# A fused linear-attention, gated-MLP and channel-mix kernel: normalisation sums without the mean, four outputs completed by a matmul with the identity, the gelu table loaded first, a branch hint, and a new hand-written order

## The chip, the cores and the metric

One core of one Trainium2 chip. The metric is the device time of one execution in microseconds, the median of several runs; lower is better. A second number is the span of one profiled execution: from its first to its last instruction.

## What is computed

Three layers follow each other on (batch 2, 768 tokens, 384 features). All inputs are float32 or, for the weights, float64, which arrive as pairs of 32-bit words; the results must hold to float32.

```python
for t in range(S):                                   # attention, 8 heads of 48
    y[:, :, t] = r_t @ (state + (u * k_t) v_t^T)     # u: the "present token's part"
    state = w_t[:, None] * state + k_t v_t^T
h = gelu_tanh(x @ w_in);  u, v = halves of h         # gated MLP, 2 x 512
v_n = (v - mean(v)) / sqrt(var(v) + 1e-6) * g_ln
x = x + (u * (w_sg @ v_n + b_sg)) @ w_out
k = relu(mix_k(x, x_prev) @ w_k) ** 2                # channel mix, 1024 wide
out = sigmoid(mix_r(x, x_prev) @ w_r) * (k @ w_v)
```

If some input lies outside the ranges for which the fast form is exact, a flag is set and a slow general form (`general`) runs after it; with the inputs used here it does not run.

## The kernel before

**Tiles.** Tokens are cut into four groups of 384 (g = 0 to 3; two batches times two halves). Attention works on 16 units (a group and a pair of heads) and 12 packs (a group and a third of its features, decays and keys). Chunks of 128 tokens are handled by matmuls; the state is carried by scans on VectorE (DVE). Every matmul of the later layers is done three times, with the high and low parts of its operands (`mm3`, lines 196 to 198), to keep float32 precision: so ScalarE (ACT) casts a high part of each operand and DVE subtracts to get the low part.

**Order.** Nothing is scheduled by the compiler: the string `ORDER` is a list of tokens, each token is one small step (`act`, line 624), and each engine runs its instructions in the order in which the tokens stand. A token names a step and the unit, pack, weight piece or tile it works on: for instance `L` loads a pack's decays, `6` moves 16 rows of a pack into the tile `six` by two DMAs (line 286), `T A P S I J` are the attention matmuls of a unit, `n` the present token's part (DVE, `t1 = pa * vT`), `O` the store of a unit (`store`, line 400), `o` six small DMAs that share a unit's rows among three features (`xT<-t1`, lines 404 and 405), `v` and `u` the first MLP matmul and its gelu, `M` the second (over tokens), `W` the third, `E`, `R`, `Z` the channel mix. `e` is a matmul on zeros and ones whose result nobody reads; it only keeps TensorE at work. All DMAs are issued by the queue of SyncE (SP), one after the other.

**Unit's output.** `outer` (I) opens a PSUM tile `py` and adds the state's part, `inner` (J) adds the part inside a chunk, and `store` (O) adds `t1` on DVE while it moves `py` to SBUF.

**Normalisation.** `mm1_v` is one generator, stepped by its token: matmuls; gelu on ACT with the row sum; on GpSimd (POOL) the sum is turned into minus the mean (line 439); ACT squares with that as its bias (line 442) and sums; POOL makes the factor by a power (lines 443 to 445); ACT applies it (line 450); ACT casts the high part into `vn_hi` (line 452); DVE makes `vn_lo`. `vn_hi` and `vn_lo` are one buffer for both batches: the second batch's casts wait until the first batch's last `M` has read it, and `M` of the second batch needs six of them.

**PSUM.** `v`, `u`, `M`, `W`, `E` and `e` share three buffers, so a matmul group waits until ACT or DVE has emptied the one three before it.

**End.** After the last output, the flag columns are summed (line 659), reduced by a matmul and compared (line 663); each engine loads the flag into a register (line 665) and branches (line 667) past the body of `general`, which holds over a thousand instructions, to a block of semaphore settings and the closing barriers.

Of the kernel before, what the change touches and what calls it, by code (L numbers as in the profile page):

```python
# [36 lines left out]
ORDER = """L1 L0 e C0.l e q0 e V0 e Q e D1 C3.l e w0 e D0 p1 q1 e e C1.l a0 p0 e C0.x j0 e C0.b e g0 e e e e C0.t e f0 e d0 e e C0.h e C0.r e K0 A0 C0.q  # L37
a1 C0.o 60 j1 g1 e e e e m0 f1 P0 C3.x T0 n0 C3.b V1 k0 e C3.t w1 e S0 K1 C3.h L2 d1 q2 P1 c0 C2.l C1.x T1 61 s0 C1.b A1 x0 C3.o n1 k1 C1.t e
V2 I0 m1 C1.r C1.h S1 C1.q D2 J0 c1 C1.o p2 s1 w2 e O0 e L3 x1 e a2 e K2 e e j2 C2.x e g2 P2 I1 C2.b f2 d2 J1 C2.t 62 n2 C2.r T2 C2.h D3 V3
C2.q A2 w3 O1 k2 L4 C3.r a3 S2 C2.o q3 p3 j3 m2 C3.q P3 C8.l c2 g3 A3 s2 T3 f3 n3 x2 D4 e e e k3 e m3 I2 p4 a4 S3 K3 j4 J2 d3 c3 P4 g4 w4 L5  # L40
T4 s3 V4 f4 q4 C8.x A4 p5 O2 k4 C4.l C8.b x3 S4 m4 c4 e C8.t I3 D5 C8.h J3 s4 n4 x4 63 C8.o e e d4 p6 e I4 w5 a5 V6 O3 A5 q5 j5 C4.x g5 o3 T5
C4.b f5 J4 m5 k5 C4.t S5 O4 C4.r w6 C4.h K4 e C4.q e C6.l C4.o e P5 K5 64 c5 d5 X0.1.h P6 L6 X0.2.h s5 C5.l X0.0.h A6 65 n6 x5 X0.1.l T6 V5
m6 I5 k6 C6.x X0.2.l S6 C6.b J5 c6 X0.0.l C6.t s6 w7 C6.h e e q6 C5.x p7 T7 C6.o x6 C5.b A7 n5 k7 C5.t P7 O5 C5.h C5.r m7 S7 C5.q C7.l I6
C5.o L7 c7 D6 V7 v0.2 C6.r s7 C6.q C9.l q8 K6 p8 x7 a6 C7.x j6 C7.b J6 g6 v0.2 v0.0 w8 C7.t f6 d6 C7.h C7.r n7 v0.2 C10.l C9.x O6 A8 q7 C7.q
C9.b V8 P8 C7.o v0.0 m8 I7 C8.r D7 C8.q C23.l T8 C9.t v0.0 a7 J7 C10.x j7 C10.b p9 g7 C9.r v0.1 66 k8 C9.q C10.t C11.l K7 C9.h C10.r w9 d7
C10.h L8 S8 C10.q n8 67 A9 C23.h C9.o c8 C10.o P9 q10 v0.0 O7 V10 s8 v0.2 u0.0 o7 v0.0 C11.x m9 v0.2 x8 v0.0 u0.1 D8 u0.0 v0.1 C11.b T9 K8
u0.1 C11.t I8 p10 a8 v0.2 k9 C11.h S9 j8 C11.r C23.o v0.1 J8 C11.o g8 C11.q u0.3 w10 O8 c9 f8 d8 f7 P10 s9 68 u0.3 A10 x9 n10 T10 V9 m10 v0.1
C24.l I9 k10 p11 v0.1 A11 v0.1 J9 n9 S10 C24.x V11 O9 P11 w11 m11 c10 L9 T11 q9 s10 L11 u0.2 C24.b x10 C16.l C24.t n11 k11 V13 C24.r I10
C15.l X1.0.h D9 u0.2 C13.l S11 X1.2.h X1.0.l J10 p12 c11 a9 X1.2.l X1.1.h v1.0 s11 C24.q X1.1.l x11 j9 K9 g9 C16.h P12 v1.0 C16.o u1.3 d9 f9
C15.h L10 O10 q11 C15.o v1.0 I11 w12 D11 C22.l C13.h T12 u1.3 C13.o J11 k12 D10 u1.2 69 O11 p13 K10 o11 v1.0 K11 P13 a10 u1.2 j10 g10 v1.0  # L50
S12 C22.h v1.1 n13 c12 a11 d10 f10 V12 w13 s12 610 C22.o A13 x12 j11 v1.0 C21.l P14 v1.1 m13 p14 T13 n12 A12 g11 k13 V14 v1.1 C20.l S13 m12 B
I12 C21.h c13 d11 u1.1 f11 s13 C21.o x13 A14 u1.1 J12 v1.1 C20.h T14 O12 w14 v1.1 C17.l m14 u1.0 k14 n14 v1.1 V15 I13 u1.0 C25.l C20.o 611
S14 C17.h J13 C17.o c14 C26.l v1.2 s14 w15 C18.l O13 x14 C25.x C25.b p15 C25.t T15 C25.r X2.1.h C29.l P15 C25.q X2.1.l k15 v2.1 X2.2.h n15
C18.h X2.2.l X2.0.h C18.o v1.2 X2.0.l C12.l A15 v2.1 S15 m15 I14 v1.2 v2.0 c15 C12.h s15 v2.1 C12.o x15 C14.l J14 I15 v1.2 O14 v2.0 v2.2 v1.2
C14.h v1.2 v2.1 C14.o J15 v2.0 C30.l v2.2 M0.3 O15 o15 v2.2 v2.0 M0.1 M0.3 | M0.3 C24.h C25.h C24.o C25.o C26.x C29.x C26.b C29.b v2.2 C26.t
C29.t u2.2 C26.h M0.1 C29.h C26.r C26.o M0.1 C26.q C19.l C29.o u2.1 C30.x u2.2 C30.b C30.t C30.h M0.2 C30.o u2.1 C19.h C19.o C27.l M1.2 M0.2
M0.2 C27.x C27.b C27.t C27.h C27.r C27.o C27.q C28.l M1.3 M1.2 M1.2 C28.x C28.b M1.0 C28.t M1.3 C28.h C28.r C28.o M1.3 C28.q C31.l C29.r
C29.q C32.l C30.r u2.0 M1.0 C30.q C33.l C31.x M1.0 C31.b M0.0 u2.0 C31.t C32.x C31.r C32.b C31.h C34.l C31.q C32.t C31.o C32.h C33.x C32.r
C32.o C32.q C38.l C33.b C33.t u2.3 M0.0 C33.r C33.h C34.x C35.l M0.0 C33.q C33.o M1.1 u2.3 C34.b C38.x X3.2.h C34.t X3.1.h C38.b C34.h X3.2.l
C34.r C38.t X3.0.h C39.l X3.1.l C34.q X3.0.l C38.h v3.2 C34.o v2.2 M1.1 v2.1 C35.x v2.2 v2.0 v2.1 u3.1 v3.2 C38.o M1.1 C39.x C35.b v3.1 C39.b  # L60
u3.1 C35.t C39.t v3.2 v2.0 C35.h C35.r C35.o v3.0 C39.h C36.l C35.q C39.o v3.1 u3.0 v3.2 C36.x v3.0 C36.b u3.3 C36.t v3.1 C36.r v3.2 C37.l
u3.2 v3.0 v3.2 G0.3.h G0.0.h G0.3.l C36.h G0.0.l u3.0 C36.o v3.1 C37.x u3.3 C37.b v3.1 C37.t v3.0 v3.1 C37.h v3.0 C37.o G0.1.h v3.0 C36.q
G0.1.l M3.3 u3.2 C37.r G0.2.h C42.l C37.q G0.2.l C38.r C38.q C41.l W0.0 C39.r M3.3 C39.q C40.l C42.x M3.3 C42.b C42.t M3.2 C41.x C42.h W0.0
C42.o C41.b C40.x C41.t C40.b C41.h C40.t C41.o C40.h M2.2 C40.r M3.2 C40.q C43.l C40.o M3.2 C41.r C41.q C44.l C42.r C42.q C45.l M2.1 M2.2
C43.x M2.2 C43.b C44.x C43.t C44.b C43.r C44.t C43.h C49.l C43.q W0.1 C43.o M2.1 C44.h C44.r C45.x M2.1 C44.q C47.l C45.b C44.o C45.t M3.1
W0.1 C45.r C45.h C49.x C46.l C45.q C49.b C45.o C49.t C47.x C49.h C47.b C49.o C47.t C47.h M2.0 M3.1 C47.o M3.1 C46.x C46.b C46.t C46.r C46.h
C48.l C46.q W0.2 C46.o M2.0 C47.r M2.0 C47.q C59.l M3.0 W0.2 G1.3.h G1.2.h C48.x G1.3.l G1.0.h C48.b G1.1.h C59.x G1.2.l C59.b C48.t C59.t
C48.r G1.0.l M2.3 C48.h C51.l C48.q M3.0 C59.h C48.o C49.r M3.0 C49.q C50.l C59.o G1.1.l C51.x C51.b W1.1 M2.3 C51.t C50.x C51.h H0 W1.0 W1.1
Y0.0.0.a Y0.0.2.a Y0.0.0.b Y0.0.1.a Y0.0.2.b W1.2 Y0.0.0.c Y0.0.1.b Y0.0.2.c Y0.0.1.c C50.b W1.0 E0.1 G2.0.h W1.2 G2.1.h C50.t G2.2.h
Y0.1.2.a C50.h E0.7 G2.1.l C50.r Y0.1.2.b C52.l C50.o C50.q M2.3 Y0.1.2.c E0.1 E0.3 G2.3.h C51.o E0.1 E0.7 G2.3.l C51.r E0.1 C53.l E0.7 E0.2  # L70
C51.q C52.x E0.1 E0.7 C52.b E0.3 E0.7 E0.0 C52.t E0.2 G2.0.l C52.h C53.x C52.r C52.o C53.b C52.q C54.l E0.6 E0.2 C53.t E0.2 G2.2.l C53.r E0.2
C53.h C55.l W2.0 C53.q Y0.1.0.a E0.6 C53.o Y0.1.0.b C54.x E0.6 Y0.1.0.c E0.6 W2.2 C54.b E0.6 W2.0 E0.0 C54.t E0.0 C54.h C54.r C55.x W2.1 E0.3
E0.0 C58.l C54.q W2.2 E0.0 E0.3 C55.b E0.3 Z0.0 C55.t G3.0.h W2.1 C55.r G3.2.h G3.0.l C56.l G3.1.h Y0.1.1.a E0.4 C55.h G3.1.l G3.3.h G3.2.l
Y0.1.1.b C55.q G3.3.l Z0.1 Y0.1.1.c E0.4 C55.o E0.4 C58.x E0.4 W3.0 H1 C58.b E0.4 C58.t Z0.2 W3.0 C58.h Y1.0.0.a C58.o Y1.1.0.a W3.1 C56.x
Y1.0.2.a C56.b Y1.1.2.a C56.t Z0.3 Y1.0.1.a C56.r C56.h W3.1 C57.l C56.q Y1.1.1.a E0.5 C54.o C56.o Z0.4 C57.x Y1.0.0.b C57.b E0.5 Y1.0.0.c
# [833 lines left out]
```

## Time and profile before

| | us |
|---|---|
| median of 3 runs | 361.02 (359.25 to 364.27) |
| the profiled execution | 361.11 |
| its span | 359.3 |
| TensorE busy in the span | 332.5 |
| DVE busy | 259.6 |
| ACT busy | 207.5 |

The profiled execution is 1.8 us longer than its span. A row "start us, us" of a timeline is the start from the span's beginning and the length of a merged stretch; in square brackets stands how long the engine was idle before it and what ended that. `PEld` is TensorE's weight load, and an engine's name with a q its sequencer, which waits, branches and issues.

### The profile page before, as it was taken

To read this page: it belongs to the slowest core of one execution; us is meant where nothing else is said; L and a number is where in the kernel's file an instruction comes from. 1 tells how busy PE (TensorE), PEld (TensorE's weight loads), DVE (VectorE), ACT (ScalarE), POOL (GpSimd) and SP (SyncE) were. 2 spreads that over 40 slices of the span, in tenths; PEclk is the share of its full clock that TensorE was granted. 3 is DMA by queue.
4 is the path that set the end of the run, shared out by engine and by line. 5 is a ranking of instruction groups with operands and counts; after the bars stand their busy time and mean duration, and the time that the engine had idled before them with its cause. 6 is when DMAs were issued, how large, how long until landed. Compare 5 with 4: busy or idle time off the path is not lost.

```text
span 359.3 us, 6219 instructions
## 1 busy us (share of the span) xinstructions
PE 332.5 (93%) x2166; PEld 295.5 (82%) x2171; DVE 259.6 (72%) x579; ACT 207.5 (58%) x572; POOL 40.8 (11%) x103
## 2 busy tenths in 40 slices
...
GB/s 212 206 141 188 152 207 160 214 106 167 175 134 185 102 54 31 44 163 37 58 89 88 85 57 44 47 42 31 117 23 53 0 2 66 0 2 44 24 44 33
DMA packets 22440, 32.57 MB, mean 91 GB/s; under 512 B 2944, under 2 KB 18816, under 8 KB 22400
## 3 DMA queue, kind: packets, MB, share of 16 engines
...
q14 instruction: 21, 0.17, 0.1%
...
## 4 chain that ended last, share of the span: by engine, by line
PE 62%; DVE 14%; DMA 10%; ACT 7%; issue 3%; SPq 1%; POOL 1%; DVEq 0%; ACTq 0%
PE po L550 9%; PE ps L198 5%; PE ps L196 5%; PE ps L197 5%; PE pk L198 4%; PE pk L197 4%; PE pk L196 4%; PE po L196 4%; PE po L198 4%; PE po L197 4%; DMA six<-pk 3%; DMA wt<-in_wp_dram 2%; DVE pk L271 2%; DMA vT<-in_rkv_dram 2%; PE pr L196 2%
## 5 line engine op out<-in xcount | busy, mean ns | idle before, releaser
L196 PE MATMUL ps<-wsg,vn_hi 128*128 128x384 f32 x96 | 32.8, 341 | 3.1 <-ACT uT L460 1.8
L198 PE MATMUL ps<-wsg,vn_lo 128*128 128x384 f32 x96 | 32.6, 339 | 0.1
L197 PE MATMUL ps<-wsg,vn_hi 128*128 128x384 f32 x96 | 32.5, 338 | 0.0
L198 PE MATMUL pk<-xk_hi,wk_lo 128*128 128x384 f32 x96 | 32.4, 337 | 0.0
L197 PE MATMUL pk<-xk_lo,wk_hi 128*128 128x384 f32 x96 | 32.3, 336 | 0.0
L196 PE MATMUL pk<-xk_hi,wk_hi 128*128 128x384 f32 x96 | 32.3, 336 | 0.0
L524 DVE TENSOR_TENSOR kr<-kr 128x384 f32<-128x384 f32 x32 | 17.7, 556 | 14.4 <-ACT kr L522 13.9
L529 ACT CAST kk_hi<-kr 128x384 fp32r<-128x384 f32 x32 | 16.1, 513 | 20.7 <-PE po L550 14.5
L522 ACT ACTIVATE kr<-pk 128x384 f32<-128x384 f32 x32 | 15.6, 489 | 18.0 <-PE pk L198 15.6
L553 DVE TENSOR_TENSOR rr<-po,rr 128x384 f32<-128x384 f32 x12 | 6.5, 555 | 25.5 <-PE po L198 14.1
L550 PE MATMUL po<-pl_win_hi,kk_hi 128*128 128x384 f32 x81 | 23.0, 338 | 0.0
L196 PEld LDWEIGHTS ps<-wsg,vn_hi 128*128 128x128 f32 x96 | 18.0, 188 | 3.9 <-ACT uT L460 2.1
L382 ACT COPY sx<-sc 48x144 f32<-48x144 f32 x32 | 14.5, 454 | 8.9 <-DVE sc L376 8.7
L531 DVE TENSOR_TENSOR kk_lo<-kr,kk_hi 128x384 fp32r<-128x384 f32 x32 | 17.4, 555 | 2.6 <-ACT kk_hi L529 2.2
L550 PE MATMUL po<-pl_win_lo,kk_hi 128*128 128x384 f32 x63 | 18.4, 339 | 0.0
L198 PEld LDWEIGHTS ps<-wsg,vn_lo 128*128 128x128 f32 x96 | 18.0, 188 | 0.4 <-DVE vn_lo L454 0.4
L550 PE MATMUL po<-pl_win_hi,kk_lo 128*128 128x384 f32 x54 | 18.2, 338 | 0.0
L198 PEld LDWEIGHTS pk<-xk_hi,wk_lo 128*128 128x128 f32 x96 | 18.0, 188 | 0.0
L197 PEld LDWEIGHTS pk<-xk_lo,wk_hi 128*128 128x128 f32 x96 | 18.0, 188 | 0.0
L196 PEld LDWEIGHTS pk<-xk_hi,wk_hi 128*128 128x128 f32 x96 | 18.0, 188 | 0.0
L197 PEld LDWEIGHTS ps<-wsg,vn_hi 128*128 128x128 f32 x96 | 18.0, 188 | 0.0
L365 DVE TENSOR_TENSOR am<-pA,c_sb 128x768 f32<-128x768 f32 x16 | 15.1, 947 | 3.6 <-PE pA L335 3.6
...
## 6 DMA issues: line engine op xcount, KB each, us to landing
...
```

The lines of the kernel that those rows point to most:

```text
L196: T.matmul(ps, lh, rh, start=(i == 0), stop=False)
L197: T.matmul(ps, lh, rl, start=False, stop=False)
L198: T.matmul(ps, ll, rh, start=False, stop=(i == n - 1))
L271: V.tensor_mul(pk4, pk4, u.rk.rearrange("p two (c j) -> p two c j", c=NCB))
L365: V.tensor_mul(u.am.rearrange("p h (c t) -> p h c t", c=NCB), u.pA[:, :, :TB].rearrange("p h (c t) -> p h c t", c=NCB), mask[:, None, None ...
L382: A.copy(u.sx[o:o + D, :, o:o + D], u.sc[o:o + D, :, 1:1 + NCB].rearrange("p e c -> p c e"))
L522: A.activation(kr, ps, AF.Relu)
L524: V.tensor_mul(kr, kr, kr)
L529: A.copy(hi, kr)
L531: V.tensor_sub(lo, kr, hi.bitcast(F32))
L550: T.matmul(pv[g][s], l, wv[i][r], start=st, stop=(i == KF - 1 and l is ll))
L553: V.tensor_mul(rr[g][:, s, :], pv[g][s], rr[g][:, s, :])
```

## The change

Five things are done. (1) The mean is not formed ahead of the squares: ACT squares 512 times the value minus the sum, and the constants are carried into the power and into `g_sb`, so GpSimd's step on line 439 goes; the factor's application now stands in a step of its own ahead of the buffer's allocation. (2) For units 0 to 3 the present token's part is added by TensorE, with a matmul of the identity with `t1` into `py` (`inject`, token `N`), and ACT copies `py` out in place of DVE's addition. (3) The first, dummy activation is gelu, which loads gelu's table; no second load is then made ahead of the first gelu. (4) A branch hint on all engines for the branch at the end. (5) A new `ORDER`: the same steps, four `N` more, and 35 `e` where there were 49.

```diff
-ORDER = """L1 L0 e C0.l e q0 e V0 e Q e D1 C3.l e w0 e D0 p1 q1 e e C1.l a0 p0 e C0.x j0 ...
+ORDER = """L0 q0 e Q e L1 e q1 e V0 e C0.l e D0 w0 e e a0 p0 e j0 K0 e g0 e e e e d0 f0 ...
...
+INJ = 4
...
-    A.activation(warm, half, AF.Tanh)
+    A.activation(warm, half, AF.Gelu_apprx_tanh)
...
+        def inject(u):
+            T.matmul(u.py, ident, u.t1, start=False, stop=False)
+
         def store(u):
+            if u.i < INJ:
+                A.copy(xT[u.g][:R, u.p, 1:] if u.p < NP - 1 else u.t1, u.py)
+                return
             V.tensor_add(xT[u.g][:R, u.p, 1:] if u.p < NP - 1 else u.t1, u.py, u.t1)
...
         A.activation(v, ps, AF.Gelu_apprx_tanh, accum_out=ln[:, 0:1])
-        G.tensor_scalar_mul(ln[:, 0:1], ln[:, 0:1], -1.0 / DH)
         yield
         t = w2.tile([P, DH], BF16, name=f"vj_{n}", tag="sg")
-        A.activation(t, v, AF.Square, bias=ln[:, 0:1], accum_out=ln[:, 1:2])
-        G.tensor_scalar(ln[:, 2:3], ln[:, 1:2], 1.0 / DH, EPS, ALU.mult, ALU.add)
-        G.tensor_tensor(ln[:, 2:3], ln[:, 2:3], half, ALU.pow)
-        G.tensor_tensor(ln[:, 3:4], ln[:, 0:1], ln[:, 2:3], ALU.mult)
+        A.activation(t, v, AF.Square, scale=-float(DH), bias=ln[:, 0:1], accum_out=ln[:, 1:2])
+        G.tensor_scalar_add(ln[:, 1:2], ln[:, 1:2], EPS * DH ** 3)
+        G.tensor_tensor(ln[:, 2:3], ln[:, 1:2], half, ALU.pow)
+        G.tensor_scalar(ln[:, 3:4], ln[:, 0:1], -1.0 / DH, ln[:, 2:3], ALU.mult, ALU.mult)
+        yield
+        A.activation(v, v, AF.Identity, bias=ln[:, 3:4], scale=ln[:, 2:3])
         yield
         if g - g % NB not in vn:
...
-        A.activation(v, v, AF.Identity, bias=ln[:, 3:4], scale=ln[:, 2:3])
-        yield
         A.copy(hi, v)
...
+            G.tensor_scalar_mul(g_sb, g_sb, float(DH) ** 1.5)
...
     order.close()
+    tc.mark_branch_hint_location("range", "LikelyTaken", mybir.ALL_ENGINES)
     flagged = nc.values_load(fi, min_val=0, max_val=1)
     ctx.close()
-    with tc.If(flagged != 0):
+    with tc.If(flagged != 0, label="range"):
```

**Three places in the new order.** First, the start of ACT's program. Before:

```order
L905 UNCONDITIONAL_BRANCH
L123 ACT_TABLE_LOAD
L123 ACTIVATE warm_69<-half_67 128x1
L352 COPY wps1_144<-pk_0_1_185 112x48x3
L352 COPY wps0_143<-pk_0_0_195 112x48x3
```

Now:

```order
L914 UNCONDITIONAL_BRANCH
L914 BRANCH_PREFETCH_HINT
L124 ACT_TABLE_LOAD
L124 ACTIVATE warm_69<-half_67 128x1
L353 COPY wps0_143<-pk_0_0_190 112x48x3
L280 ACTIVATE wt_0_0_160,over_110<-wt_0_0_160,lim_tanh_71 128x3x128
```

The hint stands at the very start of the program, some 3,500 instructions ahead of the branch it belongs to (on each engine, behind the jump into the block); the table load behind it is the only one ahead of the sigmoid's, where before a second stood ahead of the first gelu.

Second, the queue of SP around the rows of pack 5 (`pk_1_2`), the last that unit 7 waits for. Before (`xT0<-t1` are the six DMAs of unit 3's `o`; four that repeat are left out):

```order
L404 DMA xT0_83<-t1_0_0_3_493 16x384
L405 DMA xT0_83<-t1_0_0_3_493 16x384
L304 DMA vk_0_1_2_676<-in_vt_dram 128x288
L158 DMA winu0_0_raw_685<-in_w_in_dram 128x512
L286 DMA six_147<-pk_1_1_499 16x1158 x2
L248 DMA wt_2_0_702<-in_wp_dram 128x388
L158 DMA winv2_768_raw_707<-in_w_in_dram 128x512
L286 DMA six_147<-pk_1_2_593 16x1158 x2
L300 DMA vT_0_1_1_729<-in_rkv_dram 112x384
```

Now (four that repeat are left out behind the two `xT0` rows):

```order
L159 DMA winu0_0_raw_555<-in_w_in_dram 128x512
L287 DMA six_147<-pk_1_1_480 16x1158 x2
L287 DMA six_147<-pk_1_0_385 16x1158 x2
L305 DMA vk_0_1_1_626<-in_vt_dram 128x288
L249 DMA wt_2_0_630<-in_wp_dram 128x388
L159 DMA winv2_768_raw_641<-in_w_in_dram 128x512
L301 DMA vT_0_1_2_646<-in_rkv_dram 112x384
L305 DMA vk_0_1_2_649<-in_vt_dram 128x288
L411 DMA xT0_83<-t1_0_0_3_465 16x384
L412 DMA xT0_83<-t1_0_0_3_465 16x384
L287 DMA six_147<-pk_1_2_608 16x1158 x2
L301 DMA vT_0_1_1_719<-in_rkv_dram 112x384
```

Between the last `xT0` row of `o` and the move of `pk_1_2` stood five other steps (a weight piece `vk`, `win_u`, the move of `pk_1_1`, decays and `win_v`); now nothing stands between them, and these steps stand ahead of `o`.

Third, ACT between the casts of the second batch (`vn2_hi`); the groups 2 and 3 are v_2 and v_3, and `ga0`, `wk` and `uT3` are operands of later steps. Before, from the cast of v_3_2 to that of v_3_0, the last:

```order
L452 CAST vn2_hi_1719<-v_3_2_2152 128x512
L442 ACTIVATE vj_3_0_2253,ln_3_0_2218<-v_3_0_2217,ln_3_0_2218 128x512
L481 CAST ga0_3_hi_2259<-uT0_3_90 128x384
L481 CAST ga0_0_hi_2262<-uT0_0_87 128x384
L174 CAST wk1_hi_2119<-wk1_0_x_2215 128x256
L460 ACTIVATE uT3_0_1808<-pu_3_0_2204 128x384
L450 ACTIVATE v_3_1_2200<-v_3_1_2200,ln_3_1_2201 128x512
L460 ACTIVATE uT3_3_1811<-pu_3_3_2222 128x384
L452 CAST vn2_hi_1719<-v_3_1_2200 128x512
L450 ACTIVATE v_3_0_2217<-v_3_0_2217,ln_3_0_2218 128x512
L174 CAST wk1_hi_2119<-wk1_256_x_2271 128x256
L452 CAST vn2_hi_1719<-v_3_0_2217 128x512
```

Now, from the square of v_3_2 to behind the last cast:

```order
L449 ACTIVATE vj_3_2_2207,ln_3_2_2192<-v_3_2_2191,ln_3_2_2192 128x512
L454 ACTIVATE v_3_1_2169<-v_3_1_2169,ln_3_1_2170 128x512
L175 CAST wk1_hi_2070<-wk1_256_x_2178 128x256
L459 CAST vn2_hi_2121<-v_3_1_2169 128x512
L467 ACTIVATE uT3_0_1778<-pu_3_0_2197 128x384
L459 CAST vn2_hi_2121<-v_3_0_2142 128x512
L454 ACTIVATE v_3_2_2191<-v_3_2_2191,ln_3_2_2192 128x512
L467 ACTIVATE uT3_2_1780<-pu_3_2_2216 128x384
L459 CAST vn2_hi_2121<-v_3_2_2191 128x512
L467 ACTIVATE uT3_3_1781<-pu_3_3_2231 128x384
L175 CAST wk1_hi_2070<-wk1_512_x_2241 128x256
L488 CAST ga0_1_hi_2252<-uT0_1_88 128x384
```

The two `ga0` casts now stand behind the last cast of `vn2_hi`, the last cast is that of the last chunk (v_3_2) and no longer that of v_3_0, and the gelu of u_3_1 (`uT3_1`) has gone to a place behind these rows.

## Rows read from the trace of the kernel before

**Rows 1.** Busy time by engine in three stretches, with the granted clock (PEclk).
```profile
core 0: us, PE busy (x) PEld busy (x) DVE busy (x) ACT busy (x) POOL busy (x), PEclk, DMA share, GB/s
0.00:58.00 58.00, 47.65 (x391) 29.67 (x397) 50.37 (x105) 31.35 (x94) 9.76 (x39) 0.95 0.65 182
58.00:137.00 79.00, 74.56 (x596) 59.40 (x596) 59.15 (x115) 60.76 (x168) 22.18 (x46) 1.00 0.51 140
137.00:352.60 215.60, 210.28 (x1182) 206.46 (x1180) 149.93 (x360) 115.36 (x313) 8.87 (x18) 1.00 0.17 49
```

**Rows 2.** By line: busy us, mean ns of one, idle before it and its releaser.
```profile
L400 DVE TENSOR_TENSOR xT<-py,t 112x384 f32<-112x384 f32 x12 | 6.6, 546 | 2.8 <-PE py L397 2.8
...
L633 PE MATMUL idle<-d1pat 128*128 128x512 bf16 x44 | 13.8, 459 | 1.7 <-POOL d1pat L117 1.4 <-issue 0.3
...
L339 PE MATMUL pa<-pk,blku 112*112 112x384 f32 x24 | 10.5, 518 | 2.3 <-DVE pk L275 1.7 <-DVE d1w L264 0.5
...
L442 ACT ACTIVATE vj<-v,ln 128x512 bf16<-128x512 f32 x12 | 8.6, 716 | 3.3 <-POOL ln L439 3.3
...
L481 ACT CAST ga_hi<-uT 128x384 fp32r<-128x384 f32 x16 | 7.5, 508 | 0.0
...
L438 ACT ACT_TABLE_LOAD x1 | 1.3, 1283 | 0.0
```

**Rows 3.** The DMA queue of SP in order of time, 38 to 51 us.
```profile
39.58 0.53 SPq L404 DMA_DIRECT2D xT<-t  x1
...
47.23 1.14 SPq L286 DMA_DIRECT2D six<-pk  x2
```

**Rows 4.** DVE in order of time, 40 to 52 us: the products of pack 5.
```profile
43.86 0.95 DVE L271 TENSOR_TENSOR pk<-pk,rk 128x768 f32<-128x768 f32 x1
```

**Rows 5.** TensorE in order of time, 40 to 58 us.
```profile
44.89 0.94 PE L335 MATMUL pA<-pk 48*128 48x128 f32 x12
...
51.67 0.79 PE L324 MATMUL ptr<-c_sb,six 112*128 112x112 f32 x3 [2.11 <-DMA six<-pk]
52.39 1.66 PE L335 MATMUL pA<-six 48*128 48x128 f32 x12
```

**Rows 6.** Busy time and granted clock behind that wait, columns as in rows 1.
```profile
51.70:58.50 6.80, 6.80 (x37) 5.01 (x38) 5.24 (x12) 4.95 (x16) 0.00 (x0) 0.50 0.55 165
```

**Rows 7.** TensorE in order of time, 175 to 182 us.
```profile
177.87 0.44 PE L196 MATMUL ps<-wsg,vn_hi 128*128 128x384 f32 x1 [1.77 <-ACT uT L460]
...
180.99 0.45 PE L196 MATMUL ps<-wsg,vn_hi 128*128 128x384 f32 x1 [1.29 <-ACT vn_hi L452]
```

**Rows 8.** ScalarE in order of time: first cast of the second batch, and a square.
```profile
164.28 1.66 ACT L452 CAST vn_hi<-v 128x512 fp32r<-128x512 f32 x3
...
169.81 0.72 ACT L442 ACTIVATE vj<-v,ln 128x512 bf16<-128x512 f32 x1 [2.50 <-POOL ln L439]
```

**Rows 9.** GpSimd in order of time: the minus mean that this square waited for.
```profile
167.01 2.76 POOL L439 TENSOR_SCALAR ln<-ln 128x1 f32<-128x1 f32 x1 [33.61 <-ACT v L438]
...
172.72 0.22 POOL L439 TENSOR_SCALAR ln<-ln 128x1 f32<-128x1 f32 x1 [0.65 <-ACT v L438]
```

**Rows 10.** From the first cast of the second batch to the last, columns as in rows 1.
```profile
164.28:180.94 16.66, 13.40 (x67) 11.56 (x65) 11.66 (x28) 13.83 (x36) 7.00 (x12) 1.00 0.17 46
```

**Rows 11.** TensorE, the wait for the sigmoid.
```profile
267.66 0.44 PE L196 MATMUL pr<-pl_win_lo,xr_hi 128*128 128x384 f32 x1 [0.61 <-ACT rr L539]
```

**Rows 12.** Sequencers at the end: branch (L667), the block and barriers behind it (L667, L905).
```profile
L667 SPq EVENT_SEMAPHORE  x8: 17/17/17, 357.3 to 357.9; - x8
...
L667 PEldq COMPARE_BRANCH  x1: 4297/4297/4297, 353.7 to 353.7; - x1
...
L667 SPq COMPARE_BRANCH  x1: 50/50/50, 353.9 to 353.9; - x1
L667 ACTq EVENT_SEMAPHORE  x1: 17/17/17, 357.1 to 357.1; - x1
...
L905 SPq EVENT_SEMAPHORE  x10: 17/28/28, 357.9 to 359.2; - x10
```

More of the change, by code (lines that the diff above doesn't have):

```diff
@@ L41 @@
[L41 to L52, printed above, removed]
@@ L85 @@
[L85 to L88 removed]
+ORDER = """L0 q0 e Q e L1 e q1 e V0 e C0.l e D0 w0 e e a0 p0 e j0 K0 e g0 e e e e d0 f0 e e e e L2 D1 e A0 60 T0 a1 p1 m0 P0 k0 j1 K1 g1 P1 n0 f1 e d1
@@ new lines @@
+X2.2.l v2.1 C14.h O14 s15 C14.o x15 C24.x C22.l n15 v2.2 v2.1 C24.b C24.t v2.1 C24.r I15 v2.2 C28.l v2.0 C24.q v2.2 C22.h v2.1 C22.o J15
+C25.r C15.l v2.0 M1.0 C26.l O15 C25.q o15 v2.0 v2.2 C15.h C15.o M1.2 M1.0 C27.l | M1.0 v2.0 C25.h C24.h C25.o C24.o C26.x C28.x C26.b u2.1
+C28.b C26.t C28.t C26.h M1.2 C26.r C28.h C26.o C30.l C26.q M1.3 M1.2 u2.1 C27.x C28.o C27.b C27.t C27.h C27.r C27.o C27.q C31.l C30.x C30.b
+u2.2 C28.r M1.3 C28.q C29.l C30.t M1.3 C30.h C30.o u2.3 u2.2 C31.x C31.b C31.t M0.3 u2.3 C29.x C29.b C31.h C29.t C31.o C29.h C29.r C29.o
```

89 lines of the change are left out of this document (48 added, 41 removed).

## The prediction

> **What bounds the kernel now.** I read the busy times by stretch first. From 58 us on TensorE is the bound: busy 74.56 of 79 us and 210.28 of 215.6, at granted clock 1.00 [rows 1]. In the first 58 us it is not: DVE is busy 50.37 of them, TensorE 47.65, and part of the latter is the idle matmuls (459 ns each) [rows 1, 2]. So a change to TensorE's work counts in full only behind 58 us; ahead of that, what feeds it counts.
>
> Next I looked for the places at which TensorE waits. Four are touched by the change: 2.11 us for the rows `six` of pack 5 [rows 5]; 1.77 and 1.29 us in the second batch's token matmuls [rows 7]; 0.61 us at the sigmoid's matmul [rows 11]; and the time behind the last output, where the sequencers' rows show the branch [rows 12].
>
> At the first the reader is to see the order of three times. DVE had pack 5's products ready at 43.86 + 0.95 = 44.81 [rows 4]; SP moved them only at 47.23 [rows 3]; TensorE got them at 51.67 [rows 5]. [...] At the second, ACT is the last to arrive: from the first cast of the second batch to the last it is busy 13.83 of 16.66 us [rows 10], and 2.50 of the 2.83 it idles are one wait of a square for GpSimd's minus mean [rows 8], a step that took 2.76 us that once and 0.22 us the next time [rows 9].
>
> **The change, part by part.** The sum is made against the profiled execution, 361.11 us (span 359.3 and 1.8 around it), practically the median of 361.02.
>
> *The hint.* SP's branch is done at 353.9 + 0.05, but the next event on SP stands at 357.3 and on ACT at 357.1; TensorE's own branch lasts 4.30 us, from 353.7 to 358.0 [rows 12]. Nothing is computed in between: the engines wait for the code behind the jump. From SP's first event to its last pass 359.2 − 357.3 = 1.9 us. If the code were at hand, SP would go on at about 354.1 and end at 356.0: −3.2. The bounds are 0 (a hint without effect) and −3.3; on the bad side, if the hint at the program's start makes the engines fetch one place more, one such wait, +4.3. I take −3.2: what the records show between branch and event has no other work in it. TensorE's branch would have to shorten as well, since the closing barriers need every engine.
>
> [...]
>
> *The mean's step.* GpSimd's multiplication goes (12 in all), and with it the wait of 2.50 us ahead of that square [rows 8, 9]. In the new order the two `ga0` casts (2 x 0.508 [rows 2]) no longer stand ahead of the last cast, and this cast is now that of the chunk which its consumer takes last. So ACT's chain is shorter by 2.50 + 1.0 = 3.5 us, more than TensorE's 1.77 + 1.29 = 3.06 [rows 7]. What is late next: GpSimd has three steps left between a square and the factor's application, and its first step after a long rest may again take the 2.76 us that the one after 33.61 us of rest did [rows 9]. Between the first square and its application stand now a clip, a gelu and a square on ACT, some 2 us that cover part of it (the square alone is 0.72 [rows 8]). Bounds −3.1 and 0; I take −2.6, nearer the full figure, since the chain's saving exceeds the wait.
>
> *The queue of SP.* Behind the six DMAs of `o`, which start at 39.58, stood five other steps ahead of pack 5's move at 47.23 [rows 3]. Now they stand ahead of `o`, and the move is the next entry, so its issue is bound by the products at 44.81 [rows 4]: 47.23 − 44.81 = 2.4 us earlier, which covers the wait of 2.11 [rows 5]. What is moved ahead also delays `o` and everything queued behind it; `o` waits for unit 3's output, which DVE and ACT make, so it may start no earlier than now. If the wait goes, the half clock may go too: at half the clock the matmuls take 1.66/0.94 = 1.77 times as long, so 6.80 us hold 3.84 us of full-speed work, 3.0 lost [rows 5, 6]. Together 5.1 at most. The other bound is 0: DVE is busy 50.37 of these 58 us [rows 1] and may be the next to be late, as all of pack 5's and unit 7's products pass through it. I take half, −2.5.
>
> *The sigmoid.* The matmul that waited 0.61 us for an early buffer [rows 11] now comes later in the order, behind the buffer's reader: −0.6 (bounds −0.6 and 0, or as much the other way).
>
> *The four injections.* A matmul of the same shape has no own row; the nearest is `pa`, 112x112 by 112x384 in float32, two records of 518 ns each [rows 2]: 4 x 1.04 = +4.1 us on TensorE, in the first 40 us, where it has waits and idle matmuls to give (14 of these go: 14 x 0.459 = −6.4 [rows 2]). DVE loses four additions of 546 ns, −2.2 us [rows 2], and ACT gains four copies of about 0.5 (its cast of 128x384 takes 0.508 [rows 2]), at 31.35 us busy of 58 [rows 1]. On the path: between −2.2, DVE's saving in full where DVE is the bound, and +4.1; I take 0, because ACT and the additional pass through TensorE now lie between the product and the store.
>
> *The table.* The load of 1.28 us ahead of the first gelu goes [rows 2]. It lies on ACT in a stretch in which ACT is busy 60.76 of 79 us and TensorE 74.56 [rows 1]: that slack hides it, 0. Without the slack it would be worth −1.3.
>
> *Squares and constants.* The scaling goes into instructions that are there already: 0. The factor's application moves one step ahead of its cast: 0, or a buffer's wait less.
>
> Sum: 361.1 − 3.2 − 2.6 − 2.5 − 0.6 = **352.2 us**.
>
> **The rivals.**
>
> *R1, the hint does nothing.* [...] Against it: the branch records show that fetching is all that the 3.2 us hold [rows 12]. Time: 352.2 + 3.2 = 355.4.
>
> *R2, the start stays as it is.* The wait for pack 5 is replaced by one on DVE or on the decays that now come through SP in another order, and the clock falls again. For it: DVE's 50.37 of 58 us [rows 1]. Against: the products were ready 2.4 us ahead of their move [rows 3, 4]. Time: 352.2 + 2.5 = 354.7.
>
> *R3, GpSimd's next step takes the wait over.* The step that was slow was the first after a rest of 33.61 us [rows 9]; now the addition behind the first square is the first. If it is as slow, and ACT's two moved casts are needed no later than before, TensorE waits as now. Time: 352.2 + 2.6 = 354.8.
>
> [...]
>
> [...]
>
> **How the numbers follow.** The forecast, within some 1.5 us of 352.2: 0.50. R1 0.22, R2 0.13, R3 0.09, R4 0.06. Two of the first three rivals together give 357 to 358. The low end adds the parts left out: the rest of the start's term (−2.5), DVE's saving (−2.2) and the last 0.5 of the token matmuls: 347.0. The high end, 359.5, holds any two rivals together with an injection that costs 1 to 2 us. About 2% is what a measurement of this kernel can tell from no change: below 353.8 is faster, above 368.2 slower. The forecast is below that (0.50; what of it falls above the line is about made good by cases of R1 to R3 in which another term comes out larger); R1 to R3 lie within 2% (0.44); R4 is slower (0.06).
>
> **What would show it.** Right: events of the last block on SP and ACT within a microsecond of the branch, and TensorE's branch well under 4.30 us; no wait over 0.5 us in the second batch's token matmuls, and no square that waits for GpSimd; pack 5's move issued near its products, no wait of 2 us behind it, and granted clock 1.00 between 45 and 58 us. Wrong: a branch as long as before (R1); a wait of TensorE for DVE near 50 us with a half clock behind it (R2); an application that waits 2 us or more for GpSimd (R3); granted clock below 0.8 over the first 58 us (R4).

## The result, and the profile after

The changed kernel takes **349.31 us** (median of 4 runs, 347.73 to 350.65) against 360.66 (359.25 to 364.27): a ratio of 0.967, 95% interval 0.958 to 0.975. Run a second time, without an edit, it took 348.40 us, ratio 0.9755 (0.970 to 0.981). The ratios leave out runs more than 1.5% above the fastest of the same kernel, so they need not equal the quotients of the medians beside them. It is faster; the forecast was 352.2 us with a range of 347.0 to 359.5. The profiled execution has a span of 348.3 us against 359.3. The last matmul stands at 344.35 instead of 352.37, so 8.0 of the 11.0 us of span were gained ahead of it and 3.0 behind it.

Busy time by stretch, as in [rows 1] (the third stretch ends with the last matmul):

```profile
core 0: us, PE busy (x) PEld busy (x) DVE busy (x) ACT busy (x) POOL busy (x), PEclk, DMA share, GB/s
0.00:58.00 58.00, 48.22 (x404) 30.24 (x408) 50.85 (x104) 34.83 (x102) 14.55 (x40) 0.97 0.69 191
58.00:137.00 79.00, 76.09 (x602) 62.09 (x601) 58.89 (x122) 59.11 (x166) 18.51 (x37) 1.00 0.49 136
137.00:344.60 207.60, 205.51 (x1160) 202.64 (x1158) 147.50 (x351) 116.07 (x308) 11.90 (x15) 1.00 0.17 50
```

In the third stretch TensorE now idles 2.1 us (207.60 − 205.51) where it idled 5.3 [rows 1]: most of that is the token matmuls and the sigmoid. The first stretch looks as before, with DVE at 50.85 of 58 us.

The end: the branch of TensorE, the block behind it, and the last events, against [rows 12]:

```profile
L676 SPq EVENT_SEMAPHORE  x8: 17/17/17, 346.4 to 346.9; - x8
...
L676 PEldq COMPARE_BRANCH  x1: 385/385/385, 345.6 to 345.6; - x1
...
L676 SPq COMPARE_BRANCH  x1: 70/70/70, 345.9 to 345.9; - x1
L676 ACTq EVENT_SEMAPHORE  x1: 17/17/17, 346.0 to 346.0; - x1
...
L914 SPq EVENT_SEMAPHORE  x10: 17/28/28, 347.0 to 348.3; - x10
```

The branch takes 0.385 us instead of 4.297, ACT's event stands 0.1 us behind SP's branch instead of 3.2 (357.1 − 353.9), and the closing part on SP is as long as it was (346.4 to 348.3, before 357.3 to 359.2).

The second batch's token matmuls: all that TensorE waited for from 160 to 182 us (waiting instruction, releaser, us in total, times, longest), and GpSimd's first steps there:

```profile
PE pv L199 <- DVE xs_lo L433: 1.2, 2, 0.9
```

```profile
164.41 0.66 POOL L450 TENSOR_SCALAR ln<-ln 128x1 f32<-128x1 f32 x1 [34.12 <-ACT vj L449]
...
166.32 0.22 POOL L450 TENSOR_SCALAR ln<-ln 128x1 f32<-128x1 f32 x1 [0.23 <-ACT vj L449]
```

The 1.77 and 1.29 us of [rows 7] are gone; what is left is a wait of the first MLP matmul for DVE. GpSimd's first step after a rest is again slower than the next of its kind (0.66 against 0.22 us), but far from the 2.76 of [rows 9].

The start: SP, DVE, TensorE and the clock around pack 5, against [rows 3 to 6]:

```profile
41.77 0.52 SPq L411 DMA_DIRECT2D xT<-t  x1
...
45.22 0.71 SPq L412 DMA_DIRECT2D xT<-t  x1
46.04 1.16 SPq L287 DMA_DIRECT2D six<-pk  x2
```

```profile
43.42 0.96 DVE L272 TENSOR_TENSOR pk<-pk,rk 128x768 f32<-128x768 f32 x1
```

```profile
48.48 0.46 PE L336 MATMUL pA<-six 48*128 48x128 f32 x2 [0.28 <-issue]
50.78 0.90 PE L336 MATMUL pA<-six 48*128 48x128 f32 x10 [1.84 <-issue]
```

```profile
53.20:56.50 3.30, 3.30 (x30) 2.96 (x30) 2.93 (x6) 2.54 (x9) 0.00 (x0) 0.50 0.79 267
```

The move is issued at 46.04, 1.2 us earlier than before, but 1.7 us behind the products (43.42 + 0.96 = 44.38). `o` itself now starts at 41.77, not at 39.58, because the five steps stand ahead of it. TensorE still waits 1.84 us, in the middle of the scores ("issue": the profile shows no releaser; the scores read `six`, whose two DMAs were issued last), and the clock still falls, from 53.2 to 56.5 us: 3.3 us instead of 6.8.

### The profile page after: what moved, and what is told of

Read it like the earlier page. It is cut to its first block, busy times and chain, and to the rows that moved or that the text cites. A ratio compares the mean times of both kernels' runs of the same rounds, so it can differ in the third digit from the quotient of the medians.

```text
span 348.3 us, 6211 instructions
## 1 busy us (share of the span) xinstructions
PE 329.8 (95%) x2162; PEld 295.0 (85%) x2165; DVE 257.4 (74%) x575; ACT 210.0 (60%) x575; POOL 45.0 (13%) x92
## 3 DMA queue, kind: packets, MB, share of 16 engines
q1 hardware_dynamic: 22400, 32.08, 32.6%
HBM read 27.34 MB, written 2.36 MB: 85 GB/s over the span
## 4 chain that ended last, share of the span: by engine, by line
PE 70%; DVE 8%; DMA 4%; ACT 4%; POOL 1%; issue 1%; SPq 1%; DVEq 0%; ACTq 0%
PE po L557 11%; PE ps L197 5%; PE ps L199 5%; PE ps L198 5%; PE pk L199 5%; PE pk L198 5%; PE pk L197 5%; PE po L199 4%; PE po L197 4%; PE po L198 4%; DMA vT<-in_rkv_dram 3%; PE pr L199 2%; PE pr L197 2%; PE pr L198 2%; PE pu L197 2%; PE pu L198 2%
## 5 line engine op out<-in xcount | busy, mean ns | idle before, releaser
L450 POOL TENSOR_SCALAR ln<-ln 128x1 f32<-128x1 f32 x12 | 6.3, 524 | 94.1 <-ACT vj L449 94.1
```

The source lines that it names most:

```text
L450: G.tensor_scalar_add(ln[:, 1:2], ln[:, 1:2], EPS * DH ** 3)
```

## The experiments

"At clock 1.00" below is a straight line through the 145 runs of all these kernels that list a clock, time against mean granted clock, with one slope for all (2.4 us for each 0.01 of clock): it puts the kernel before at 355.4 to 356.3 us in its four sets of runs, the changed one at 347.3 and 348.2 in its two. It is a fit, not an experiment, and the mean clock also holds the idle time at the end. The median clock was 0.981 in 55 runs of the kernel before, 0.9945 in 10 runs of the changed one.

**The hint.** First the changed kernel without it:

```diff
-    tc.mark_branch_hint_location("range", "LikelyTaken", mybir.ALL_ENGINES)
```

> The changed kernel without the branch hint. Theory (the hint had the code behind the branch at hand; it is worth what the two traces show at the end, 6.70 us from the last matmul to the end against 3.80): 349.3 + 2.9 = 352.2 us, TensorE's branch again about 4.3 us long, the last compute at the same 344.5. Rival (the shorter end comes from another program length or code layout, not from the hint): 349.3 us and a branch of under 1 us.

Measured: 352.73 us (351.46 to 354.73), ratio to before 0.983 (0.978 to 0.989). TensorE's branch:

```profile
L675 PEldq COMPARE_BRANCH  x1: 4157/4157/4157, 345.2 to 345.2; - x1
```

The long branch is back; the last matmul ends at 344.05, the span is 350.8. The start, which this edit does not touch, differs from that of the changed kernel's profile. Here TensorE does not wait for pack 5's rows. It waits 1.23 us for ACT at 47 us and then for DVE, whose product `t` waits for `vT`, the load that SP issues right behind the move; and the clock is at half for some 7 us (columns as above):

```profile
52.02 1.04 PE L340 MATMUL pa<-six,c_sb 112*112 112x384 f32 x2 [1.17 <-DVE t L372]
```

```profile
51.41 0.56 DVE L372 TENSOR_TENSOR t<-pa,vT 112x384 f32<-112x384 f32 x1 [1.55 <-DMA vT<-in_rkv_dram]
```

```profile
52.70:59.40 6.70, 6.24 (x36) 4.86 (x36) 6.34 (x12) 4.30 (x13) 0.00 (x0) 0.50 0.84 251
```

That is the sign that the prediction gave for R2, in one run. In the changed kernel's profile DVE waits 1.54 us for the same load, to 51.01, so this chain ends there at about the same time as the one through the move. Then the hint alone:

```diff
     order.close()
+    tc.mark_branch_hint_location("range", "LikelyTaken", mybir.ALL_ENGINES)
     flagged = nc.values_load(fi, min_val=0, max_val=1)
     ctx.close()
-    with tc.If(flagged != 0):
+    with tc.If(flagged != 0, label="range"):
```

> The kernel before with nothing but the hint and the label. Theory: 360.7 - 2.9 = 357.8 us, TensorE's branch about 0.4 us. [...] The time ahead of the branch the same as before, 352.6 us, within 1 us.

Measured: 357.55 us against 359.67, ratio 0.996 (0.992 to 1.000).

```profile
L668 PEldq COMPARE_BRANCH  x1: 380/380/380, 351.1 to 351.1; - x1
```

The branch is short here too, in a program that is otherwise the old one. So the hint does it, and not the layout. From the traces it is worth 2.9 to 3.0 us (from the end of the last matmul to the end of the span 6.7 and 6.8 us without it, 3.8 and 3.8 with it). The times give 1.5 us by the ratio and 2.1 by the medians for the hint alone (the interval reaches just to 2.9), and 3.4 to 4.3 for its removal, around the traces' figure.

This profile showed something else. Its order is that of before, but its wait for pack 5's rows was 1.4 us instead of 2.11 and there was no half clock at 52 us; there was one behind the token matmuls' wait instead (columns as above):

```profile
51.70:58.50 6.80, 6.80 (x52) 4.99 (x50) 6.46 (x14) 6.46 (x17) 0.21 (x1) 1.00 0.79 246
174.00:182.00 8.00, 7.46 (x25) 6.72 (x26) 4.66 (x10) 7.55 (x20) 0.00 (x0) 0.57 0.22 43
```

So the wait of the second batch can cost its own length and a stretch at half clock behind it (0.50 from 175 to 180 us here), but need not: the wait is 1.76 us here and was 1.77 in the kernel before [rows 7], where the clock stayed at 1.00. And the half clock of [rows 6] belongs to that run, not to every run of that order. Without it, the last attention matmuls stand where the changed kernel's profile, with 3.3 us of half clock, has them; with it, 4 us later. The kernel before, the changed one and the hint alone, in this order, each its last `py` row:

```profile
129.78 0.86 PE L397 MATMUL py<-am,vk 128*48 128x128 f32 x12
```

```profile
125.88 0.86 PE L398 MATMUL py<-am,vk 128*48 128x128 f32 x12
```

```profile
125.78 0.86 PE L397 MATMUL py<-am,vk 128*48 128x128 f32 x12
```

The new order shows the same two states. First the kernel without the hint above, with its long stretch at half clock, then the changed kernel with eight idle matmuls more (below), without any:

```profile
125.89 0.86 PE L398 MATMUL py<-am,vk 128*48 128x128 f32 x12
```

```profile
124.13 0.86 PE L395 MATMUL py<-am,vk 128*48 128x128 f32 x12
```

So, like with like, the new order ends the attention earlier: by 1.7 us without a half clock (125.78 and 124.13), by 3.9 with one of some 7 us (129.78 and 125.89). These are single profiles; another of the new order with such a stretch, that of the mean's step put back, has 126.90.

**The parts against the order.** All parts, with the order of before:

```diff
-ORDER = """L0 q0 e Q e L1 e q1 e V0 e C0.l e D0 w0 e e a0 p0 e j0 K0 e g0 ...
+ORDER = """L1 L0 e C0.l e q0 e V0 e Q e D1 C3.l e w0 e D0 p1 q1 e e C1.l ... N0 J0 ... N3 J3 ...
```

> The changed kernel with the order of before (the four injections put just ahead of the inner products). Theory 1 (the parts carry the token matmuls' gain, the order the start's): hint -2.9, the square's wait for GpSimd gone -2.5, start and sigmoid unchanged: about 355.3 us. Theory 2 (the order carries all but the hint): 357.8 us. Theory 3 (the injections and the table shorten the start also in the old order): 352 us or less.

Measured: 353.25 us (351.35 to 354.39), ratio 0.985 (0.979 to 0.990). TensorE's waits in the second batch:

```profile
PE ps L194 <- ACT vn_hi L456: 1.3, 1, 1.3
PE ps L194 <- ACT uT L464: 0.8, 1, 0.8
```

And the new order (without the four `N`) with the old parts:

```diff
-ORDER = """L1 L0 e C0.l e q0 e V0 e Q e D1 C3.l e w0 e D0 p1 q1 e e C1.l ...
+ORDER = """L0 q0 e Q e L1 e q1 e V0 e C0.l e D0 w0 e e a0 p0 e j0 K0 e g0 ...
```

> The kernel before with the new order, less the four injections: mean formed on GpSimd, tanh's table first, four additions on DVE, no hint. Theory 1 (the order carries the start's 3.9 us and the sigmoid's 0.9, the parts the token matmuls): 360.7 - 4.8 = 355.9 us, and again a wait of a square for GpSimd in the second batch. Theory 2 (the order carries all but the hint): 349.3 + 2.9 = 352.2 us. Theory 3 (the order is of use only with the parts): 358 us or more.

Measured: 355.12 us (354.61 to 357.63), ratio 0.990 (0.985 to 0.995).

```profile
PE pu L193 <- ACT uT L457: 1.2, 1, 1.2
PE pv L195 <- DVE xs_lo L423: 0.9, 1, 0.9
```

The parts with the hint take 1.5%, the order 1.0%; together that is 2.5%, against 2.45% and 3.3% measured for both, each known to some 0.5% or worse. Within that they add up, and neither "all is the order" nor "the order needs the parts" holds: the order's run is near Theory 1 (its square waits 1.49 us for GpSimd), the parts' run lies between Theory 1 and Theory 3. The second batch's waits for ACT are shared: with the old parts and the new order no token matmul waits, but a `pu` ahead of them does, for 1.2 us where there were 3.06; with the new parts and the old order the token matmuls still wait 2.1; only both leave nothing. The same shows on ACT. By the measure of [rows 10], from the start of the first cast to the end of the last, it took 16.66 us before, 15.5 with the order and the old parts, 15.1 with the parts and the old order, and 172.14 + 0.61 − 159.59 = 13.16 in the changed kernel:

```profile
159.59 1.14 ACT L459 CAST vn_hi<-v 128x512 fp32r<-128x512 f32 x2
...
172.14 0.61 ACT L459 CAST vn_hi<-v 128x512 fp32r<-128x512 f32 x1
```

The wait at the sigmoid goes with the order: it is 0.61 in the run with the old order, and absent in the other.

**The changed kernel again**, as the base of what follows:

> The changed kernel once more, unedited, to learn how its runs spread. A straight line through the runs so far (time against mean granted clock, one slope for all kernels) gives 2.17 us for each 0.01 of clock, and 348.3 us for this kernel at clock 1.00, 356.1 for the kernel before. Theory (the runs of both kernels differ among themselves by the stretches at half clock alone): median 349.3 us, clocks 0.99 to 1.00, single runs within 1 us of the line. Rival (the four runs so far were lucky ones): median 350.5 to 351.5 us at clocks near 0.985, as the kernel without the hint has once 1.7 to 3 us are taken off for it.

Measured: 348.40 us (348.20 to 350.63), clocks 0.986 to 1.000, median 0.994. The theory holds for the median, which is 0.9 us below it; the first four runs were not lucky.

**The mean's step.** Put back in the new order:

```diff
         A.activation(v, ps, AF.Gelu_apprx_tanh, accum_out=ln[:, 0:1])
+        G.tensor_scalar_mul(ln[:, 0:1], ln[:, 0:1], -1.0 / DH)
...
-        A.activation(t, v, AF.Square, scale=-float(DH), bias=ln[:, 0:1], accum_out=ln[:, 1:2])
+        A.activation(t, v, AF.Square, bias=ln[:, 0:1], accum_out=ln[:, 1:2])
...
```

> The changed kernel with the minus mean formed on GpSimd again (its step, the old squares and factor; the order unchanged). Theory 1 (the order by itself took 2.1 of the 3.3 us that the token matmuls gained, as the run with the order and the old parts had it): 349.3 + 1.2 = 350.5 us; a square waits 2 us or more for GpSimd on ACT, TensorE waits about 1.2 us in the second batch's token matmuls. Theory 2 (the removed step is what counts, as the prediction put it): 349.3 + 2.6 = 351.9 us. Theory 3 (ACT had slack in the new order): 349.3 us, no wait on TensorE.

Measured: 351.08 us (350.39 to 353.29): 2.7 us slower than the run above, 1.8 more than the first set. TensorE's and GpSimd's rows:

```profile
174.09 0.44 PE L197 MATMUL pu<-xs_hi,win_hi 128*128 128x384 f32 x1 [1.23 <-ACT uT L468]
```

```profile
164.46 1.69 POOL L446 TENSOR_SCALAR ln<-ln 128x1 f32<-128x1 f32 x1 [32.92 <-ACT v L445]
```

TensorE's wait of 1.2 us is Theory 1's; the time lies between Theory 1 and Theory 2, of which the trace shows only the first. And taken away in the old order, by itself:

```diff
-        G.tensor_scalar_mul(ln[:, 0:1], ln[:, 0:1], -1.0 / DH)
...
-        A.activation(t, v, AF.Square, bias=ln[:, 0:1], accum_out=ln[:, 1:2])
+        A.activation(t, v, AF.Square, scale=-float(DH), bias=ln[:, 0:1], accum_out=ln[:, 1:2])
...
```

> The kernel before with nothing but the new squares, power and factor (no step of GpSimd ahead of the square). Theory (the prediction's: 2.5 us of ACT's chain go, and TensorE's two waits of 1.77 and 1.29 us shrink by about as much): 360.5 - 2.6 = 357.9 us, no square waits for GpSimd; runs at high clock more frequent, since the kernel with the hint alone lost its clock behind these very waits (0.50 from 174 to 181 us). Rival (in the old order ACT's other work keeps the last cast where it was; it took both to bring the gain): 359.5 us or more, TensorE still waiting 2 us or more in the second batch.

Measured: 358.93 us against 359.94, ratio 0.997 (0.993 to 1.001). Its profiled run was its longest (span 360.5, three stretches at half clock), so only what happens in the second batch is read:

```profile
PE ps L196 <- ACT uT L459: 1.3, 1, 1.3
PE ps L196 <- ACT vn_hi L451: 1.3, 1, 1.3
```

```profile
170.47 2.36 POOL L442 TENSOR_SCALAR ln<-ln 128x1 f32<-128x1 f32 x1 [35.67 <-ACT vj L441]
```

```profile
166.67 1.66 ACT L451 CAST vn_hi<-v 128x512 fp32r<-128x512 f32 x3
...
181.68 0.62 ACT L451 CAST vn_hi<-v 128x512 fp32r<-128x512 f32 x1
```

No square waits for GpSimd any more, and yet the token matmuls wait 2.6 us of 3.06, and ACT needs 15.63 us from the first cast to the last, 1.0 less than before and not 2.5. Two other waits of ACT have come in place of the square's: 0.78 us for a weight piece from DVE, and 0.59 us for the factor, behind GpSimd's long step, which is now the addition after the square (2.36 us). So by the waits the rival holds; the time lies between theory and rival and does not decide.

**The injections**, left out (DVE adds units 0 to 3 again):

```diff
-INJ = 4
+INJ = 0
-... I0 C0.r s1 C0.h p2 f2 C1.x N0 m1 x1 J0 ...
+... I0 C0.r s1 C0.h p2 f2 C1.x m1 x1 J0 ...
```

> The changed kernel without the four injections: units 0 to 3 are again added up by DVE. Theory (the start is bound by the chain of loads, decays and moves, in which neither engine's share of these four additions is the last): 349.3 us, within 0.7. Rival 1 (DVE is the bound of the start, four additions of 0.55 us): 351.5 us. Rival 2 (the 4.1 us of added matmuls are on the path): 345.5 us or a little more.

Measured: 349.33 us (349.00 to 350.81), 0.9 above the run again and equal to the first set. In the trace the start is another:

```profile
18.54 0.91 PE L389 MATMUL py<-pk,sx 112*112 112x128 f32 x6 [1.05 <-ACT sx L380]
20.84 1.59 PE L337 MATMUL pa<-pk,blku 112*112 112x384 f32 x2 [1.39 <-DVE pk L273]
```

```profile
20.00:27.00 7.00, 5.85 (x42) 4.56 (x44) 6.85 (x16) 3.27 (x11) 1.00 (x3) 0.51 0.51 129
54.00:61.00 7.00, 6.40 (x37) 5.02 (x37) 6.64 (x12) 4.37 (x13) 0.00 (x0) 0.52 0.79 246
```

Two waits close together, 1.05 and 1.39 us, and the clock falls at 20 us (0.51 to 27 us); in the changed kernel there is one wait of 0.40 us there and the clock stays at 1.00 (16 to 27 us). The new order with the old parts, which has no injection either, shows the same dip (0.57 from 20 to 28 us). This profile is of the longest of the seven runs, but their clocks (median 0.988 against 0.9945) point the same way. So in this order the injections cost nothing that these runs can tell and keep the start in step, but little of that reaches the end: the attention's last matmuls stand at 128.3 there, in the profiles of the new order with injections at 124.1 to 126.9, and the medians are 0.9 us apart at most.

**The idle matmuls.** All 35 left out:

```diff
-ORDER = """L0 q0 e Q e L1 e q1 e V0 e C0.l e D0 w0 e e a0 p0 e j0 K0 e g0 e e e e d0 ...
+ORDER = """L0 q0 Q L1 q1 V0 C0.l D0 w0 a0 p0 j0 K0 g0 d0 ...
```

> The changed kernel without any of its 35 idle matmuls. Theory (they hold the clock up in the start, and it falls without them): the clock near 0.5 over 20 to 45 of the first 55 us, at 0.43 us for each at most, part of it hidden behind DVE: 353 to 362 us. Rival (TensorE's own work holds the clock up, and idle matmuls only delay it): 347 to 349.5 us.

Measured: 349.83 us (348.31 to 350.47), 1.4 more than the run again, 0.5 more than the first set. (The theory's 0.43 us is 1 − 0.94/1.66, from the score matmuls of [rows 5].)

```profile
8.00:45.00 37.00, 30.27 (x274) 20.19 (x274) 36.15 (x76) 23.20 (x71) 7.06 (x13) 1.00 0.72 201
45.00:52.00 7.00, 6.80 (x53) 5.72 (x55) 5.94 (x14) 4.77 (x14) 0.19 (x1) 0.51 0.30 70
```

Neither holds in full. The column says 1.00 from the first matmul on, but it also says so where the trace has no record of the clock yet, and the lengths of the matmuls differ from it. The first twelve score matmuls here, and the same ones in the changed kernel, where 19 idle matmuls were recorded ahead of them:

```profile
8.00 1.65 PE L332 MATMUL pA<-pk 48*128 48x128 f32 x12 [8.00 <-DVE pk L268]
```

```profile
7.88 0.94 PE L336 MATMUL pA<-pk 48*128 48x128 f32 x12 [0.28 <-DVE pk L272]
```

So TensorE's work begins at the speed of half clock (1.65 us; 1.66 at a granted clock of 0.50 in [rows 5, 6]); the next such group, at 13.70, still takes 1.27 us, the one at 23.20 takes 0.94. From some 14 us to 45 the column stays at 1.00 on TensorE's own work, without a single idle matmul, then it falls to 0.51 (45 to 52 us) behind waits of 1.19 and 1.78 us. The mean clocks of these runs, 0.975 to 0.990, are lower than those of the changed kernel (0.986 to 1.000), and they leave the first 6 us out. So the idle matmuls do serve the clock, ahead of the first work above all; of that, 0.5 to 1.4 us reach the end. Then eight more, ahead of unit 7's scores:

```diff
-... C5.r A7 j6 ...
+... C5.r e e e e e e e e A7 j6 ...
```

> The changed kernel with eight more idle matmuls, just ahead of unit 7's scores, where TensorE waits about 2 us in all for pack 5's rows and the clock then falls for 3.3 us. Theory (the wait is what lets the clock fall, and a stretch at half clock costs 0.31 us for each of its microseconds by the line through all runs): no half clock near 50 us, median clock 0.999, 348.4 - 1.2 = 347.2 us. Rival 1 (the clock falls all the same): 348.4 us at 0.994. Rival 2 (eight are too many and push the scores back): 349 us at a clock of 1.00.

Measured: 348.16 us (347.66 to 352.84), median clock 0.997.

```profile
48.35 1.90 PE L637 MATMUL idle<-d1pat 128*128 128x512 bf16 x8
50.18 1.27 PE L333 MATMUL pA<-six 48*128 48x128 f32 x12
```

```profile
44.00:58.00 14.00, 12.86 (x120) 9.04 (x120) 12.02 (x23) 9.51 (x28) 0.69 (x1) 1.00 0.57 156
```

In this profile it goes as the theory has it: the wait is filled, the scores start at 50.18, and the clock stays at 1.00 from 44 to 58 us. The runs' clocks agree: five of six are 0.996 or more, of the changed kernel's ten three. The time is 0.24 us lower, which the scatter does not tell from nothing. It is the lowest median of all these kernels, but not shown to be better than the changed one.

**SP's queue.** Unit 3's rows ahead of the five steps, one load of values (`vk`, which the text below calls keys) behind the move:

```diff
-... I4 w5 a5 ... V6 C8.b w6 O4 e e o3 ... e 65 s5 ...
+... I4 o3 w5 a5 ... V6 C8.b O4 e e ... e 65 w6 s5 ...
```

> The changed kernel with the six DMAs of unit 3's rows put five steps earlier in SP's queue and one load of keys put behind pack 5's move, so that the move is issued about 1 us earlier (45.0 us instead of 46.0; the products are ready at 44.4). Theory (the move's place in the queue sets TensorE's wait, as the prediction put it): the wait of 1.1 to 1.8 us ahead of the scores shrinks by 1, the half clock behind it goes in most runs, 347.2 us. Rival (DVE's wait for the values' load, which then comes later, or another chain ends at the same time): 348.4 us, the attention's end at 125 to 126 us as now.

Measured: 350.93 us (349.58 to 354.52), slower by 1.6 to 2.5 us.

```profile
43.10 0.53 SPq L302 DMA_DIRECT2D vk<-in_vt_dram  x1
...
45.58 1.15 SPq L284 DMA_DIRECT2D six<-pk  x2
```

```profile
45.59 0.84 PE L345 MATMUL pkv<-vk,kT 128*64 128x48 f32 x12 [3.34 <-DMA vk<-in_vt_dram]
```

The move came 0.5 us earlier, not 1, and its wait went; but another `vk`, one of the five steps, moved from 39.22 to 43.10, and TensorE waited 3.34 us for it, with half clock (0.50) from 44 to 50 us. What was put ahead on this queue was paid by what stood behind it.

**The table**, loaded twice again:

```diff
-    A.activation(warm, half, AF.Gelu_apprx_tanh)
+    A.activation(warm, half, AF.Tanh)
```

> The changed kernel with the dummy activation of before (tanh), so that gelu's table is loaded a second time, 1.28 us, ahead of the first gelu. Theory (ACT has slack there, as the prediction put it): 348.4 us, within 0.6, and the attention's end where it was, at 124 to 126 us. Rival (ACT is on the path from the first MLP matmuls on): 349.7 us, and the attention's end 1.3 us later.

Measured: 349.20 us (348.50 to 351.83), between the medians of the changed kernel's two sets of runs (348.40 and 349.31) and 0.5 below the rival. The load of 1.28 us stands at 58.44, and no wait of TensorE over 0.55 us follows it up to 78 us; its attention's last matmuls stand at 126.8, 0.9 us later than the changed kernel's, but it was 1.2 us behind at 38 us already. Theory and rival are 1.3 us apart, too close for these runs; the trace speaks for the slack.

## Why the prediction was right, and where not

The total was right: 352.2 forecast, 348.4 to 349.3 measured, on the right side and inside the range, 3 to 4 us below the sum. The 11.0 us between the spans of the two profiles are 3.9 up to the end of the attention, 2.95 from there to the last token matmul, 1.2 from there to the last matmul, and 3.0 behind it; the sum had 2.5, 2.6, 0.6 and 3.2. The terms fared differently.

*The hint* (−3.2): right. 2.9 to 3.0 us by the traces, in both orders. R1 falls by the two runs: with a hint that the engines execute at 0.7 to 0.8 us of the span, TensorE's branch at 345.6 takes 0.385 us, without it 4.157. That the engines wait for code there agrees with the traces ([rows 12] show only the time): before, all that the DMA queues move between SP's branch and ACT's event (353.95 to 357.1 us) is five packets of instructions, 0.05 MB, which start at 354.6 to 354.9, the longest of them 2.0 us long, to 356.6; in the changed kernel no instructions are moved from 344.4 to 346.0, and over the whole span it has 35 such packets instead of 40.

*The token matmuls* (−2.6): the figure was right. The 3.06 us went, a wait for DVE of some 0.5 us more came, and the way from the last attention matmul to the last token matmul is 2.95 us shorter. The sum on ACT was right too: 16.66 − 13.16 = 3.50 us, as forecast. What failed in it is the step that adds the wait of 2.50 us and the casts' 1.0 as two savings, each its own: by itself the removed step shortens ACT's stretch by 1.0 us and TensorE's waits by 0.5 (2.6 left), since ACT then waits elsewhere; by itself the order shortens the stretch by 1.2 and the waits by 1.8. They need each other: the casts and gelus that ACT does in between must be out of the way before the missing step shows in full. R3 holds in half: GpSimd's slow step did change its place (2.36 us for the addition that is now first, in the old order), but the factor's application waited only 0.59 us for it, and in the changed kernel the addition took 0.66 us.

*The queue of SP* (−2.5): the step that failed is "so its issue is bound by the products at 44.81". The five steps that were moved ahead of `o` delayed `o` by 2.2 us, and the move with it: it was issued at 46.04, 1.7 us behind the products, 1.2 us earlier and not 2.4, and the wait was 1.84 us and not gone. The prediction said of this only that `o` "may start no earlier than now". R2, DVE as the next to be late, was close: in the run without the hint it is DVE that TensorE waits for, with the half clock behind it. The attention still ended 3.9 us earlier in the two profiles, more than forecast, but not for that reason: the profile before has a longer stretch at half clock (6.8 us against 3.3), and, like with like, the new order ends the attention 1.7 to 3.9 us earlier. What in the order does this is not shown, and that a term with a failed ground came out near its size is luck.

The clock was also better in general. The medians of all runs (360.05 us in 55, 348.45 in 10) differ by 11.6 us, the fitted line at clock 1.00 gives 7.2 to 8.9; the rest goes with the clock (0.981 against 0.9945), a part of which is only the shorter idle end. Which of the edits makes stretches at half clock rarer is not shown: the parts in the old order, with the hint, have a median clock of 0.9935 already, the new order with the old parts 0.986, the hint alone 0.988. The injections take away the stretch at 20 us, but it is the new order that has it without them; in the profile of the kernel before there was none at that place.

*The sigmoid* (−0.6): right, by the order alone. Between the last token matmul (211.41 before, 204.56 after: 6.85 us) and the last matmul (8.0 us) another 1.2 us came; 0.61 of it is this wait, 0.5 is less busy time of TensorE there (138.66 against 139.16 us), which no run explains.

*Injections and table* (0 each): right within what the runs tell: without either, the medians (349.33 and 349.20) lie 0.9 and 0.8 us above one set of the changed kernel's runs and at the other. That the clock in the start would go with the injections (1.00 from 16 to 27 us with them, 0.51 from 20 to 27 in the profile without) was not foreseen.

*R4, slower by the clock*: falls. The changed kernel's granted clock is 0.97 over the first 58 us, where the sign for R4 was below 0.8. Without any idle matmul the first twelve score matmuls take 1.65 us where they take 0.94 at a granted clock of 1.00 [rows 5], then, from some 14 us to 45, the clock column stays at 1.00 with nothing but TensorE's own work, and the time is 349.83 us. So in that run the idle matmuls are not the larger part of what holds the clock up.
